# Heads sorted into slots at run time, with band-only work for five slots when at most three heads retrieve

## The chip, the cores and the metric

The kernel runs on one core of one Trainium2 chip. The metric is the device time of one execution in microseconds (us); all times below are us unless marked ns. The engines are named as the profile names them: PE is TensorE (PEld its weight loads), DVE is VectorE, ACT is ScalarE, POOL is GpSimd, and SP is the engine whose queue issues nearly all transfers.

## The reference

Attention for 4 batches and 8 heads with 768 positions of 64 elements, then a feed-forward layer on the 3072 joined rows. A head that is marked in `is_retrieval` sees all earlier positions; the others see only the first `n_sink` = 4 positions and a window of the last `window` = 64:

```python
causal = rel >= 0                                   # rel = query position - key position
stream_keep = causal & ((key < n_sink) | (rel < window))
mask = causal if is_retrieval[head] else stream_keep
a = softmax(where(mask, q @ k.T / 8, -1e9)) @ v     # per batch and head
x = a.transpose(0, 2, 1, 3).reshape(3072, 512)
out = maximum(x @ w1, x @ w2) @ w_out               # w1, w2: 512 x 1024; w_out: 1024 x 512
```

`is_retrieval` is an input and holds 1, 0, 1, 0, 0, 0, 1, 0: three of eight heads retrieve. The numbers `n_sink` and `window` are known when the program is built; the flags are not.

## The kernel before

**Attention.** Heads are worked on in pairs (`pair(b, p)`, 16 of them). A pair loads q, k and v for two heads in three transfers of 384 KB on SP's queue (L357, nine buffers `ld`), casts them to bf16 (`qb` and `vb`, on POOL for nearly all pairs), transposes q and k on PE (L373) and copies them out of PSUM as `qt` and `kz`. Scores are computed with keys on the partitions, in six steps for every head (the list `FULL`), each filling a PSUM buffer of up to 512 columns out of three (`sc`): three "near" steps that hold two key blocks next to the diagonal each, and three "far" ones. Together they are the whole causal triangle. ACT takes the exponential into `at` (L405). A head that doesn't retrieve is masked in two ways: in the far steps the bias of the exponential is -30000 unless the head retrieves (`bias_j`, and `bias_0`, which spares the first four keys); in the near steps DVE multiplies with a mask `msk` that is built for each head out of the flags (L267). So every head costs the same, whatever its flag. PE multiplies with v, 65 columns at a time (the 65th is a column of ones for the sum of the softmax, L429, PSUM `po`), DVE divides (L440, L441, into `xs`), and PE transposes the result (L452) into `xt`, which the dense part reads.

**Dense part.** It uses maximum(x w1, x w2) = relu(x (w1 - w2)) + x w2. `wd_bf` = w1 - w2 is computed once (L306), and `wm` = w2 w_out, too (transposes at L315, matmuls at L326). Per batch there are two groups of 384 rows, each with 32 matmuls "up" (L468), eight relus (L474 on ACT, L476 on DVE) into `gt`, and for each 128 rows four matmuls with `wm` (L484), eight with w_out (L490), a copy `ot` and a transfer to the output (L496).

**Order.** Nothing is ordered by hand. Each operation is entered into a plan (`Plan.op`) with a cost for each engine that can do it, its predecessors, its buffers and a priority. `Plan.schedule` then walks through time: the operation that can start first is taken, and among those that can start at the same time the one with the lowest priority number. This settles the order of instructions on each engine when the program is built. On the chip each engine goes through its list in that order and waits by semaphore where it must. Attention has low numbers, dense work has 1000 and more, so dense matmuls fill what attention leaves free.

**Constants.** The flags `ir` are loaded by ACT's queue (L240) beside the first q, k and v, and only the masks and biases depend on them (L257, L259, L261, L267).

Of the kernel before, what the change touches and what calls it, by code (L numbers as in the profile page):

```python
# [8 lines left out]
F32 = mybir.dt.float32  # L9
# [140 lines left out]
def kernel(  # L150
# [12 lines left out]
):  # L163
    nc = tc.nc
# [6 lines left out]
    scale = 1.0 / float(D) ** 0.5  # L171

# [11 lines left out]
    def tl(name, shape, dt=BF16, n=None):  # L184
        if n is None:
            return sb.tile(shape, dt, name=name, tag=name)
        return Pool([sb.tile(shape, dt, name=f"{name}{i}", tag=f"{name}{i}") for i in range(n)])

    def psum(name, n):
        return Pool([pp.tile([128, 512], F32, name=f"{name}{i}", tag=f"{name}{i}") for i in range(n)])  # L190
# [3 lines left out]
    row = tl("row", [128, 1], F32)  # L194
    causal = tl("causal", [128, 256], F32)
# [3 lines left out]
    ir = tl("ir", [128, H, 2], I32)  # L199
    nsf = tl("nsf", [128, H], F32)  # L200
    bias_j = tl("bias_j", [128, H], F32)
    bias_0 = tl("bias_0", [128, H], F32)
    msk = tl("msk", [128, H, 2, 256])
    w2_bf = tl("w2_bf", [128, KC, d_ff])
    wd_bf = tl("wd_bf", [128, KC, d_ff])
    wo_bf = tl("wo_bf", [128, FC, d_model])
    w2t = tl("w2t", [128, FC, d_model])
# [5 lines left out]
    ld = tl("ld", [128, 2, NB, D], F32, 9)  # L213
    qb_p = tl("qb", [128, NB, 2, D], BF16, 4)
    vb_p = tl("vb", [128, 2, NB, D + 1], BF16, 3)
    qt_p = tl("qt", [128, S], BF16, 3)
    kz_p = tl("kz", [128, 2, S], BF16, 3)
    at_p = tl("at", [128, 512], BF16, 12)
    rz_p = tl("rz", [128, NB], F32, 4)
    xs_p = tl("xs", [128, NB, d_model], BF16, 2)  # L220
    xt_p = tl("xt", [128, KC, S], BF16, 3)
    gt_p = tl("gt", [128, FC, GT], BF16, 2)
    ot_p = tl("ot", [128, d_model], F32, 3)
    sc_p = psum("sc", 3)
    po_p = psum("po", 2)
    mm_p = psum("mm", 3)

    P = Plan()

    def copy(e, o, i):  # L230
        if e == "ACT":
            nc.scalar.copy(out=o, in_=i)  # L232
        else:
# [4 lines left out]
    ir_handle = _dc.replace(is_retrieval.tensor, dtype=I32, shape=(2 * H,))  # L238
    ir_ap = bass.AP(tensor=ir_handle, offset=0, ap=[[0, 128], [1, 2 * H]])
    d_ir = P.op(lambda e: nc.scalar.dma_start(out=ir, in_=ir_ap.rearrange("p (h t) -> p h t", t=2)),  # L240
                {"ACT": 0.45}, prio=-100, size=0.3)
    c_rel = P.op(lambda e: nc.gpsimd.iota(rel, pattern=[[1, 256]], base=0, channel_multiplier=-1,
                                          allow_small_or_imprecise_dtypes=True), {"POOL": 0.5}, prio=-100)
    c_row = P.op(lambda e: nc.gpsimd.iota(row, pattern=[[1, 1]], base=0, channel_multiplier=1,
                                          allow_small_or_imprecise_dtypes=True), {"POOL": 0.3}, prio=-99)
    c_id = P.op(lambda e: nc.vector.tensor_scalar(
        out=ident, in0=rel[:, 0:128], scalar1=0.0, scalar2=None, op0=ALU.is_equal),
        {"DVE": 0.25}, [c_rel], prio=-50)
    c_ca = P.op(lambda e: nc.vector.tensor_scalar(
        out=causal, in0=rel, scalar1=0.0, scalar2=None, op0=ALU.is_ge), {"DVE": 0.22}, [c_rel], prio=-49)  # L250
    c_fa = P.op(lambda e: nc.vector.tensor_scalar(
        out=far, in0=rel, scalar1=float(window), scalar2=None, op0=ALU.is_ge), {"DVE": 0.22}, [c_rel], prio=-48)
    c_ns = P.op(lambda e: nc.vector.tensor_scalar(
        out=nsink, in0=row, scalar1=float(n_sink), scalar2=None, op0=ALU.is_ge), {"DVE": 0.1}, [c_row], prio=-47)
    c_f0 = P.op(lambda e: nc.vector.tensor_scalar_mul(out=far0, in0=far, scalar1=nsink),
                {"DVE": 0.3}, [c_fa, c_ns], prio=-46)
    c_nf = P.op(lambda e: nc.vector.tensor_scalar_add(out=nsf, in0=ir[:, :, 0], scalar1=-1.0),  # L257
                {"DVE": 0.1}, [d_ir], prio=-45)
    c_bj = P.op(lambda e: nc.vector.tensor_scalar_mul(out=bias_j, in0=nsf, scalar1=-NEG),  # L259
                {"DVE": 0.1}, [c_nf], prio=-44)  # L260
    c_b0 = P.op(lambda e: nc.vector.tensor_scalar_mul(out=bias_0, in0=bias_j, scalar1=nsink),  # L261
                {"DVE": 0.1}, [c_bj, c_ns], prio=-43)
    c_mk = []
    for h in range(H):
        def f(e, h=h):
            for m in range(2):
                nc.vector.scalar_tensor_tensor(  # L267
                    out=msk[:, h, m, :], in0=(far0 if m == 0 else far), scalar=nsf[:, h:h + 1],
                    in1=causal, op0=ALU.mult, op1=ALU.add)
        c_mk.append(P.op(f, {"DVE": 0.8}, [c_nf, c_f0, c_ca], prio=h + 0.3))  # L270

    init = []
    for i, t in enumerate(kz_p.tiles):
        for hh in range(2):
            init.append(P.op(lambda e, t=t, hh=hh: nc.vector.memzero(t[64 - 64 * hh:128 - 64 * hh, hh, :]),
                             {"DVE": 0.5}, prio=-40 + 30 * i))
    for i, t in enumerate(vb_p.tiles):
        init.append(P.op(lambda e, t=t: nc.gpsimd.memset(t[:, :, :, D:D + 1], 1.0),
                         {"POOL": 0.2}, prio=-40 + 30 * i))
    kz_init = init  # L280
# [3 lines left out]
    d_w = {}  # L284

    def load_weights(prio):
        for i, (name, arr, rows) in enumerate((("w2", moe_w2, KC), ("wo", moe_w_out, FC), ("w1", moe_w1, KC))):
            n = rows // 4
            for c in range(4):
                dst = w_raw[{"w1": 0, "w2": 1, "wo": 2}[name]][:, c * n:(c + 1) * n, :]  # L290
                src = arr[c * 128 * n:(c + 1) * 128 * n, :].rearrange("(c p) f -> p c f", p=128)
                d_w[name, c] = P.op(lambda e, dst=dst, src=src: nc.sync.dma_start(out=dst, in_=src),
                                    {"SP": 0.45}, prio=prio + 0.1 * i + 0.01 * c, size=0.524, rate=0.39)

    wd_ops, w2_ops, wo_ops, wm_ops, w2t_ops = [], [], [], [], []

    def prep_weights():
        for c in range(4):
            w2_ops.append(P.op(lambda e, c=c: copy(e, w2_bf[:, c, :], w_raw[1][:, c, :]),
                               {"DVE": 0.62, "ACT": 0.95}, [d_w["w2", c]], prio=40 + c))  # L300
        for c in range(4):
            wo_ops.append(P.op(lambda e, c=c: copy(e, wo_bf[:, 2 * c:2 * c + 2, :], w_raw[2][:, 2 * c:2 * c + 2, :]),
                               {"DVE": 0.62, "ACT": 0.95}, [d_w["wo", c]], prio=44 + c))
        for c in range(4):
            def f(e, c=c):
                (nc.vector if e == "DVE" else nc.gpsimd).tensor_sub(  # L306
                    out=wd_bf[:, c, :], in0=w_raw[0][:, c, :], in1=w_raw[1][:, c, :])
            wd_ops.append(P.op(f, {"DVE": 1.15, "POOL": 2.6}, [d_w["w1", c], d_w["w2", c]], prio=48 + c))
        for fch in range(FC):
            bk = Buf(mm_p)  # L310

            def tr(e, fch=fch, bk=bk):
                psb = bk.t.bitcast(BF16)
                for c in range(KC):
                    nc.tensor.transpose(psb[:, c * 128:(c + 1) * 128],  # L315
                                        w2_bf[:, c, fch * 128:(fch + 1) * 128], ident)
            o = P.op(tr, {"PE": 0.23}, w2_ops + [c_id], [bk], prio=300 + fch)
            w2t_ops.append(P.op(lambda e, fch=fch, bk=bk: copy(e, w2t[:, fch, :], bk.t.bitcast(BF16)[:, 0:d_model]),
                                {"DVE": 0.34, "ACT": 0.48}, [o], [bk], prio=52 + fch))
# [14 lines left out]
    def near(j):  # L334
        return (j, 128 * j, min(256, S - 128 * j), 256 * (j % 2))

    FULL = (
        ("near", [near(0), near(1)]),
        ("far0", [(0, 256, 512, 0)]),
        ("near", [near(2), near(3)]),  # L340
        ("far", [(1, 384, 384, 0), (3, 640, 128, 384)]),
        ("near", [near(4), near(5)]),
        ("far", [(2, 512, 256, 0)]),
    )

    xs, xt, xt_ops = {}, {}, {}

    def pair(b, p):
        r = b * HP + p
        h0 = 2 * p  # L350
        if p == 0:
            xs[b], xt[b], xt_ops[b] = Buf(xs_p), Buf(xt_p), []
        raws, loads = [], []
        for i, src in enumerate((q, k, v)):
            t = Buf(ld)
            raws.append(t)
            loads.append(P.op(lambda e, t=t, src=src: nc.sync.dma_start(  # L357
                out=t.t, in_=src[b, h0:h0 + 2].rearrange("h (n p) d -> p h n d", p=128)),
                {"SP": 0.45}, (), [t], prio=r + 0.01 * i, size=0.393, rate=0.225))
        bfs = []  # L360
        qt, kz, vb = Buf(qt_p), Buf(kz_p), Buf(vb_p)
        tops = []
        for i in range(2):
            t = Buf(qb_p)
            o = P.op(lambda e, t=t, i=i: copy(e, t.t.rearrange("p n h d -> p h n d"), raws[i].t),
                     {"POOL": 0.83, "DVE": 0.5} if r < 2 else {"POOL": 0.83}, [loads[i]], [raws[i], t],
                     prio=r + 0.01 * i)
            bk = Buf(mm_p)

# [131 lines left out]
    for b in range(B):  # L501
        for p in range(HP):
            pair(b, p)
# [41 lines left out]
```

The softmax here doesn't subtract the row's maximum and nothing guards it: scores larger than these inputs give would overflow.

## Time and profile before

| what | before |
|---|---|
| time, median of 3 runs (lowest to highest) | 221.69 us (221.56 to 222.52) |
| profiled execution, span | 221.9 us |
| PE busy | 199.0 us (90%), 1888 matmuls |
| ACT busy | 151.2 us (68%) |
| DVE busy | 122.7 us (55%) |
| POOL busy | 48.9 us (22%) |
| read from memory, written | 25.17 MB, 6.29 MB |
| packets under 512 bytes | 75,216 of 80,357 |

The busy time of an engine is a mean over stages with different limits. To see what bounds the kernel, the table of slices is read, in which every digit is the busy share of one fortieth of the span, then the chain of waits, which follows the work back from the last instruction, and then busy times of single stages. Rows of groups have the form: line, engine, operation, out <- in, shape, count | busy time, mean ns of one | idle time of the engine before them and what ended it. The costliest groups by their busy time are the scores at L398 (58.4), the exponentials at L405 (115.9 over all forms), the matmuls at L490 (46.5), L468 (46.3), L429 (38.5) and L484 (24.6).

### The profile page before, as it was taken

The page shows a single profiled execution, that of the slowest core. Times are in us where ns is not written, and L with a number is a line of the kernel's source. Part 1 is how long each engine was busy: PE and PEld are TensorE (multiplying, and loading weights), DVE is VectorE, ACT ScalarE, POOL GpSimd, SP SyncE. Part 2 cuts the span into 40 slices and gives each one's busy share as a digit, 9 for nine tenths or more (in the row PEclk, how much of TensorE's full clock was granted, in tenths as well). Part 3 has the DMA queues.
Part 4 walks back from the last instruction along what each step waited for, and adds up shares of the span by engine and source line. Part 5 has one row for each costly group of instructions (what it writes and reads, how often), then busy time and mean ns, then how long its engine had stood idle before and what let it go on. Part 6 is the DMA issues. An engine that isn't in the chain of part 4 may idle for free.

```text
span 221.9 us, 4796 instructions
## 1 busy us (share of the span) xinstructions
PE 199.0 (90%) x1888; PEld 125.7 (57%) x1888; DVE 122.7 (55%) x298; ACT 151.2 (68%) x291; POOL 48.9 (22%) x59
## 2 busy tenths in 40 slices
PE   0267986799999999999999999999999999999993
PEld 0245564366667677677767767755545454554541
DVE  6978999993799888988986876730000000000000
ACT  2158997675988989999989999933527253352721
POOL 1374015853542441364231100000000000000000
PEclk9999999799999999999999999999999999999999
DMA  5999999999999999999401011012021120302112
GB/s 122 219 218 316 345 321 379 227 221 198 230 212 219 206 231 241 261 226 246 75 3 47 3 47 52 0 40 96 9 97 47 47 95 4 124 17 95 47 47 95
DMA packets 80357, 31.76 MB, mean 143 GB/s; under 512 B 75216, under 2 KB 75216, under 8 KB 80336
## 3 DMA queue, kind: packets, MB, share of 16 engines
q1 hardware_dynamic: 80192, 31.46, 61.1%
q8 instruction: 14, 0.23, 0.4%
q14 instruction: 7, 0.06, 0.1%
q10 hardware_dynamic: 144, 0.01, 0.0%
HBM read 25.17 MB, written 6.29 MB: 142 GB/s over the span
## 4 chain that ended last, share of the span: by engine, by line
PE 69%; DVE 23%; ACT 3%; issue 2%; DMA 1%; ACTq 0%; DVEq 0%
PE mm L490 18%; PE mm L468 16%; PE sc L398 11%; PE mm L484 9%; PE po L429 7%; DVE at L417 4%; PE mm L326 4%; DVE msk L267 3%; DVE xs L441 3%; PE mm L373 3%; DVE kz L234 3%; DVE at L413 2%; DVE at L421 1%; DMA ir<-in_is_retrieval_dram 1%; PE mm L452 1%
## 5 line engine op out<-in xcount | busy, mean ns | idle before, releaser
L398 PE MATMUL sc<-qt,kz 128*128 128x128 bf16 (+2 forms) x320 | 58.4, 285 | 2.6 <-DVE kz L234 1.8
L405 ACT ACTIVATE at<-sc 128x512 bf16<-128x512 f32 (+1 forms) x96 | 55.3, 576 | 1.0 <-PE sc L398 0.5
L490 PE MATMUL mm<-wo_bf,gt 128*128 128x512 bf16 x192 | 46.5, 379 | 0.0
L468 PE MATMUL mm<-xt,wd_bf 128*128 128x384 bf16 x256 | 46.3, 326 | 0.0
L429 PE MATMUL po<-vb,at 128*128 128x65 bf16 x672 | 38.5, 195 | 4.1 <-DVE at L417 1.7
L429 PEld LDWEIGHTS <-at 128*128 128x128 bf16 x672 | 31.8, 98 | 14.5 <-DVE at L417 4.7
L405 ACT ACTIVATE at<-sc,bias_j 128x512 bf16<-128x512 f32 x64 | 38.2, 598 | 2.3 <-PE sc L398 1.9
L232 ACT COPY ot<-mm 128x512 f32<-128x512 f32 x22 | 12.9, 587 | 37.5 <-PE mm L490 37.5
L398 PEld LDWEIGHTS <-kz 128*128 128x128 bf16 x320 | 28.7, 100 | 16.8 <-issue 2.8
L234 POOL CAST qb<-ld 128x768 bf16<-128x768 f32 x32 | 29.9, 948 | 31.8 <-DMA ld<-in_q_dram 11.5
L468 PEld LDWEIGHTS <-wd_bf 128*128 128x128 bf16 x256 | 23.9, 98 | 14.7
L474 ACT ACTIVATE gt<-mm 128x384 bf16<-128x384 f32 x51 | 25.1, 493 | 5.9 <-PE mm L468 5.6
L490 PEld LDWEIGHTS <-gt 128*128 128x128 bf16 x192 | 17.9, 98 | 19.2
L373 PE MATMUL mm<-ident,qb 128*128 128x128 bf16 x192 | 17.1, 230 | 11.2 <-POOL qb L234 11.2
L484 PE MATMUL mm<-wm_bf,xt 128*128 128x512 bf16 x96 | 24.6, 379 | 0.0
L405 ACT ACTIVATE at<-sc,bias 128x512 bf16<-128x512 f32 x32 | 22.4, 700 | 1.4 <-PE sc L398 1.2
L234 POOL CAST vb<-ld 128x768 bf16<-128x768 f32 x16 | 13.7, 858 | 42.9 <-PE po L429 38.1
L373 PEld LDWEIGHTS <-qb 128*128 128x128 bf16 x192 | 12.8, 103 | 12.8 <-POOL qb L234 11.8
L417 DVE TENSOR_TENSOR at<-at,msk 128x512 bf16<-128x512 bf16 x32 | 19.2, 600 | 1.5 <-ACT at L405 1.3
L413 DVE TENSOR_TENSOR at<-at,msk 128x512 bf16<-128x512 bf16 x32 | 16.1, 503 | 6.0 <-ACT at L405 5.8
L441 DVE TENSOR_TENSOR xs<-po,rz 128x384 bf16<-128x384 f32 x32 | 17.8, 558 | 1.1
L234 DVE COPY kz<-mm 64x768 bf16<-64x768 bf16 x23 | 12.6, 547 | 3.1 <-PE mm L373 2.9
(43 smaller groups left out, 137.0 us busy)
## 6 DMA issues: line engine op xcount, KB each, us to landing
ld<-in_q_dram SPq DMA_DIRECT2D x16, 384.0 KB, 6.2
ld<-in_k_dram SPq DMA_DIRECT2D x16, 384.0 KB, 6.3
ld<-in_v_dram SPq DMA_DIRECT2D x16, 384.0 KB, 6.3
out_dram<-ot SPq DMA_DIRECT2D x24, 256.0 KB, 2.0
raw<-in_moe_w_dram SPq DMA_DIRECT2D x8, 512.0 KB, 6.7
raw<-in_moe_w_out_dram SPq DMA_DIRECT2D x4, 512.0 KB, 8.6
ir<-in_is_retrieval_dram ACTq DMA_DIRECT2D x1, 8.0 KB, 3.3
```

The source lines that it names most:

```text
L234: (nc.vector if e == "DVE" else nc.gpsimd).tensor_copy(out=o, in_=i)
L373: nc.tensor.transpose(psb[:, n * 128:(n + 1) * 128], t.t[:, n].rearrange("p h d -> p (h d)"), ident)
L398: nc.tensor.matmul(sc.t[:, off:off + w], lhsT=kz.t[:, hh, j * 128:(j + 1) * 128], rhs=qt.t[:, q0:q0 + w], start=True, stop=True, skip_grou ...
L405: nc.scalar.activation(out=at.t[:, 0:n], in_=sc.t[:, 0:n], func=ACT.Exp, scale=scale, bias=bias)
L413: nc.vector.tensor_mul(out=a, in0=a, in1=m)
L417: nc.vector.tensor_mul(out=a, in0=a, in1=m)
L429: nc.tensor.matmul(po.t[:, i * (D + 1):(i + 1) * (D + 1)], lhsT=at.t[:, off + t * 128:off + (t + 1) * 128], rhs=vb.t[:, hh, j, :], start=( ...
L441: nc.vector.tensor_tensor(out=xs[b].t[:, :, h * D:(h + 1) * D], in0=p3[:, :, 0:D], in1=rz.t.unsqueeze(2).to_broadcast([128, NB, D]), op=AL ...
L468: nc.tensor.matmul(bk.t[:, 0:GT], lhsT=wd_bf[:, c, f * 128:(f + 1) * 128], rhs=xt[b].t[:, c, g * GT:(g + 1) * GT], start=(c == 0), stop=(c ...
L474: nc.scalar.activation(out=gt.t[:, f, :], in_=bk.t[:, 0:GT], func=ACT.Relu)
L484: nc.tensor.matmul(bk.t, lhsT=xt[b].t[:, c, c0:c0 + 128], rhs=wm_bf[:, c, :], start=(c == 0), stop=False)
L490: nc.tensor.matmul(bk.t, lhsT=gt.t[:, f, t * 128:(t + 1) * 128], rhs=wo_bf[:, f, :], start=False, stop=(f == FC - 1))
```

## The change

The change uses the flags to leave work out, and not only to mask it. A head that doesn't retrieve needs only the blocks around the diagonal and the first four keys. Since the flags are known at run time only, the program holds two versions of the whole work and picks one with a branch.

- **Sorting.** DVE counts the flags and computes a permutation `perm` that puts the heads that retrieve first. Each engine reads the count into a register and branches (`tc.If(few <= FULL_SLOTS)`, FULL_SLOTS is 3).
- **At most three retrieve.** Slots 0 to 2 do the full triangle; slots 3 to 7 do the band alone, in three steps with smaller blocks (`BAND`: 448, 384 and 320 columns), and their four sink keys in one step of 512 columns for both heads of a pair. SP reads the eight head numbers into registers. The load of a pair becomes one transfer per head with the address from a register, and so do the loads of w1 and w2, whose rows are put into the order of the slots: 64 rows each.
- **More than three.** The full triangle for all heads, with loads by pair as before. It is not run with these flags.
- **Around it.** w_out is loaded ahead of the branch; the flags are loaded by SP's queue. The relu outputs and `w2t` lie in the memory of the raw weights, which makes room. `at` has eight buffers rather than twelve, and the band steps have `as` with three each. The exponentials are chained, so that their planned order is kept. The matmuls with w_out come ahead of those with `wm` in the dense part. Copies of sink keys and values for the band heads are made on POOL.

```diff
+    FULL_SLOTS = 3
+    narrow = window <= 64 and 0 < n_sink <= 32
+    WN = 192
...
+        nc.sync.dma_start(out=ir, in_=ir_ap.rearrange("p (h t) -> p h t", t=2))
+        for c in range(4):
+            load_weight("wo", c)
...
+        V.tensor_scalar(out=irn, in0=ir, scalar1=0.0, scalar2=None, op0=ALU.not_equal)
+        V.tensor_tensor(out=flag, in0=irn[:, :, 0], in1=irn[:, :, 1], op=ALU.max)
+        V.tensor_tensor_scan(out=count, data0=one, data1=flag, initial=0.0, op0=ALU.mult, op1=ALU.add)
...
+            V.tensor_reduce(out=perm[:, 0:H], in_=hot, axis=mybir.AxisListType.X, op=ALU.add)
+        V.tensor_copy(out=perm[:, H:H + 1], in_=nr)
...
+        BAND = (
+            ("band0", [(0, 0, 256, 0), (1, 128, WN, 256)]),
+            ("band1", [(2, 256, WN, 0), (3, 384, WN, 256)]),
+            ("band2", [(5, 640, 128, 0), (4, 512, WN, 128)]),
+        )
...
+                if rows:
+                    two = []
+                    for hh in range(2):
+                        two.append(P.op(lambda e, t=t, src=src, hh=hh: nc.sync.dma_start(
+                            out=t.t[:, hh], in_=src[b, bass.ds(head(s0 + hh), 1)].rearrange(
+                                "o (n p) d -> p (o n) d", p=128)),
+                            {"SP": 0.5}, (), [t], prio=r + 0.01 * i, size=0.197, rate=0.225))
...
+                o = score_op([(0, 256, S - 256, 0)], lambda j: ks.t, qt, [ks], tops + [ok], 2 * r + 0.15, sc)
+                o = exp_op(sc, ats, lambda t: t, S - 256, None, [o], 2 * r + 0.15)
...
-                o = P.op(d0, {"PE": 0.865}, xt_ops[b] + wm_ops, [bk, xt[b]], prio=1000 + 100 * b + 10 * g + 5 + t)
...
+                    o = P.op(d0, {"PE": 0.865}, [o] + xt_ops[b] + wm_ops, [bk, xt[b]],
+                             prio=1000 + 100 * b + 10 * g + 3 + t)
...
+    few = nc.values_load(perm[0:1, H:H + 1], min_val=0, max_val=H,
+                         skip_runtime_bounds_check_because="a count of H flags")
+    with tc.If(few <= FULL_SLOTS) as branch:
+        _, at = nc.values_load_multi_w_load_instructions(
+            perm[0:1, 0:H], engines=(mybir.EngineType.SP,), min_val=0, max_val=H - 1,
+            skip_runtime_bounds_check_because="a permutation of the heads")
+        run([s < FULL_SLOTS for s in range(H)], lambda s: at[s], True, flags_by_slot)
+    with branch.Else():
+        run([True] * H, lambda s: s, False, flags_by_head)
```

## The prediction, on record before the run

> **What bounds the kernel now.** I read the table of slices first, then the chain of waits, then busy time by stage. In the slices (40 of 5.55 us; one digit is the busy share in tenths):
>
> ```profile
> PE   0267986799999999999999999999999999999993
> ACT  2158997675988989999989999933527253352721
> DMA  5999999999999999999401011012021120302112
> ```
>
> TensorE is full from slice 10 to the end, the loads stop after slice 19, and ScalarE is nearly full until slice 26. The chain gives the stage borders: the first dense matmul starts at 53.65, and only matmuls follow at the end. From the timeline and the last pieces of the chain (start us, us, what):
>
> ```profile
> 53.65 0.81 PE L468 MATMUL mm<-xt,wd_bf 128*128 128x384 bf16 x4
> ```
>
> ```profile
> 205.16 5.20 PE mm L468 x32
> 210.36 0.86 PE mm L484 x4
> 211.22 1.73 PE mm L490 x8
> ...
> 218.21 0.58 ACT ot L232
> ```
>
> So there are three stages: up to 53.65 (attention of batch 0 and preparing weights, at the pace of the loads), 53.65 to 147 (attention mixed with dense work), 147 to 218.2 (dense alone); then 3.7 for the last copy and its transfer. Busy us by stage (length, then PE, PEld, DVE, ACT, POOL):
>
> ```profile
> 0.00:53.65 53.65, 36.60 (x397) 24.14 (x398) 47.51 (x104) 34.24 (x63) 23.06 (x29) 0.97 1.12 260
> 53.65:147.00 93.35, 91.26 (x1121) 65.47 (x1120) 73.92 (x192) 86.81 (x171) 25.87 (x31) 1.00 0.69 140
> 147.00:218.25 71.25, 71.13 (x374) 36.09 (x372) 1.25 (x3) 29.61 (x58) 0.00 (x0) 1.00 0.16 63
> ```
>
> A busy PE is not yet a PE at its peak, so I price matmuls by the chain instead: four of 384 columns take 0.65, four of 512 take 0.865, 42 of 65 take 1.29, six transposes 0.335. Each is columns / 2.4 GHz plus 2 to 4 ns. By the order in the program the mixed stage holds 1118 matmuls with 200,440 columns: 83.5 us, plus 1118 x 2.7 ns = 86.5. It lasts 93.35, so **7 us of it are stalls**. The last stage holds 374 with 168,704 columns: 70.3 + 1.0 = 71.3 of 71.25. After 53.65 the kernel is bound by TensorE's columns.
>
> [...] The queue SP shows both faces of that, an issue into an empty queue and one held back:
>
> ```profile
> 0.74 0.43 SPq L357 DMA_DIRECT2D ld<-in_q_dram  x1
> ...
> 59.74 1.69 SPq L357 DMA_DIRECT2D ld<-in_q_dram  x1
> 61.52 1.68 SPq L357 DMA_DIRECT2D ld<-in_k_dram  x1
> ```
>
> A load of 384 KB comes every 1.78; issuing needs 0.43 of it. The rest is the pace of the transfers.
>
> **The change, part by part.**
>
> 1. Fewer columns. is_retrieval has three ones, so the branch with three full slots runs. A full head has 10 score matmuls (2688 columns) and 21 for the output (L429); a band head 6 (1152 columns) and 15; each of the three pairs with a band head adds one of 512 for the sinks. Scores: 320 to 12x10 + 20x6 + 12 = 252, 86,016 to 32,256 + 23,040 + 6,144 = 61,440 columns. Output: 672 to 12x21 + 20x15 = 552, 7,800 columns fewer. Together 32,376 / 2400 + 188 x 2.7 ns = 14 us less PE. That which falls after the first dense matmul is gain; that before lies in the loads' shadow.
>
> 2. ScalarE. Exponentials go from 192 (115.9 us by the sum of rows at L405) to 144: 72 full ones at the same mean of 604 ns = 43.5, sixty band ones taken at 0.56, 0.50 and 0.49 (rows of 512, 384 and 256 give the bounds 0.61 and 0.49) = 31, twelve of 512 for the sinks = 7.3; 82. Beside that six more copies of kz at 0.79. In the mixed stage the rows add up to 112 before (87 of exponentials, the rest relus and copies) where the stage shows 86.8 busy, since the rows' durations overlap: a factor of 0.77. After, they add up to 86 (58 of exponentials from the middle of pair 4 on, 15 copies of kz, xt and qt, 18 relus, six ot): 66 busy of a stage of 76. ScalarE goes from 93% to 87% and doesn't take over.
>
> 3. VectorE. Masks: 128 products to 108 shorter ones; ten fewer of the msk instructions (10 x 0.47 = 4.7 us at the start), 11 small ones more for sorting the heads, smk and zeroing, which lie between the branch and the landing of pair 0's k (about 6 us of VectorE work in a gap of 7). GpSimd gets 48 copies of four columns or partitions and about ten clears; it was busy 26 of 93 in the mixed stage, which hides them.
>
> 4. The start. Loads of q, k and v now wait for the flags. ir landed at 4.0; then 11 dependent small VectorE instructions (nsf, bias_j, bias start 0.20 apart; the three of 64 elements taken at 0.25, between the 0.17 of 8 elements and the 0.35 of 256) = 2.4; then SP reads a register, branches, and reads eight more. No row shows such a read. [...] **first load at 8.5**, range 7.5 to 11, against 0.74. Queued behind it on SP is every load, behind those everything. w_out (2 MB) fills the wait: at the 340 GB/s of the slices it needs 6.2.
>
> 5. The way to the first dense matmul. In the built order it stands behind the transposes of pair 5's q and k (before: of pair 4's). Before, 17 loads and 6.3 MB of weights come first: 0.74 + 17x1.78 + 18.5 + 2 for landing = 51.5; the cast of pair 5's k did start at 51.19. After: 8.5 + 17x1.78 + 4.2 MB / 343 GB/s = 12.2, + 2 = 53.0. Cast 0.83, transposes 0.5 and 12 short matmuls: **first dense matmul at 55**. w1's differences and wm lie before that: w1 lands near 39, two differences at 2.4 on GpSimd end near 44.
>
> 6. The issue. 48 loads become 96 halves, 8 of w1 and w2 become 16, each with a register address and one register instruction more. The stream has 0.89 per half. The static issue of 0.43 is the lower bound; twice that plus the register work, 1.2, the upper. I take 0.6, hidden.
>
> 7. The mixed stage. 918 matmuls with 162,190 columns: 67.6 + 2.5 = 70.1, plus stalls between 0 (ScalarE is freer) and 15 (shorter bursts, each with its own chain of score, exponential, mask, output); I take 6: **76**. Pair 15's k stands 59 us into the stage, near 114; it lands by 8.5 + 12.2 + 47x1.78 + three stores at 1.7 + 2 = 111.5. The loads end just in time.
>
> 8. The last stage. 390 matmuls with 175,872 columns: 73.3 + 1.0 = **74.3**. L490's matmuls now come ahead of L484's, so at the last group nothing stands between the last relu and its reader: one relu (0.49) and its signals, 1.
>
> Sum: 55 + 76 + 74.3 + 1 + 3.7 = **210.0 us**, 5.3% below 221.69.
>
> **The rivals.**
>
> - Stalls grow: with half-filled bursts the order planned ahead fits less, and the mixed stage has 15 us of stalls. 55 + 85 + 74.3 + 1 + 3.7 = 219. For it: loads end just in time, three score buffers stay. Against it: ScalarE and VectorE have more room than before.
> - Stalls vanish: 55 + 70 + 74.3 + 3.7 = 203. For it: ScalarE at 93% was the likeliest cause of the 7 us. Against it: PE's order is fixed, and any late transfer stops it.
> - The issue becomes the bound: at 1.2 per half the first dense matmul comes at 8.5 + 50x1.2 + 2 + 2 = 72.5, and pair 15 is 10 pairs x 6 x 1.2 = 72 behind pair 5 rather than 59, so 72.5 + 89 + 74.3 + 1 + 3.7 = 240, **slower**. The break-even is near 1.03 per half. For it: no register-addressed DMA is in this trace. Against it: the bare issue takes less than half of the room.
>
> **How the numbers follow.** Main case 0.57 (206 to 214), stalls grow 0.20 (214 to 222), stalls vanish 0.10, issue as the bound 0.13 (part of it between 222 and 240). Range 202.5 to 221: it leaves out the slow issue and the edges of the second and third. Faster 0.85, same 0.02, slower 0.13.
>
> **What would show it.** Right: the first row of L541 on SP at 8 to 9; pitch of the halves near 0.89 with short issues when the queue is empty; the first up matmul (L616) near 55; 252 score and 552 output matmuls in the page; the last output matmul near 131; then dense alone for 74 us. Wrong: halves over 1 us apart with the DMA slices below 9 (the issue binds); PE digits of 7 and 8 in the mixed stage with waits for exponentials or masks (stalls); a first load after 11 (the register reads are mispriced).

## The result, and the profile after

The changed kernel takes **219.29 us** (median of four runs, 218.64 to 220.31) against 221.89 for the kernel before beside it (221.56 to 222.52): a ratio of 0.988, 95% interval 0.984 to 0.993. The forecast was 210.0. The direction was right and the time lies in the range, but the gain is 1.2% where 5.3% had been forecast. Medians and ratios here are of fast executions alone; the one profile of a slow one is that of e6_two_queues (228.37 us at a mean granted clock of 0.944, where its fast ones took 223.41 to 226.70 at 0.961 to 0.962), so its landmark in the table below may be late for that reason too.

First the table of slices, now 40 of 5.46 us; PEclk is the TensorE clock that was granted, in tenths, and GB/s what the transfers moved:

```profile
PE   0029767699789999998999999999999999999990
ACT  0738878335988989977899887625426263442621
PEclk9999995769999999999999999999999999999999
DMA  5999999999999999999995111012021120202121
GB/s 170 307 221 219 221 232 235 225 181 223 219 199 225 206 230 191 221 240 225 232 247 121 51 48 52 0 54 96 0 96 48 51 96 32 113 4 96 48 89 67
```

Counting slices from 0, TensorE's digit is only 6 or 7 in slices 4 to 7 (22 to 44 us), and its granted clock drops to 0.5 to 0.7 in slices 6 to 8 (33 to 49 us). The DMA engines read as busy all the time up to slice 20; their digit doesn't show at which rate they work. GB/s does: w1 and w2 are on their way in slices 4 to 7, at 221 to 235 (in e1_full below, the same weights at full width come at 357, at a DMA share of 1.02 against 1.06 here). Next, from the timeline, the first dense matmul, which the forecast had put at 55 (start us, us, what):

```profile
62.52 0.81 PE L617 MATMUL mm<-xt,wd_bf 128*128 128x384 bf16 x4
```

and busy us by stage, with borders set as in the forecast, at the first dense matmul and at the last matmuls of the attention (length, then PE, PEld, DVE, ACT, POOL, granted clock, DMA share, GB/s):

```profile
0.00:62.52 62.52, 38.52 (x393) 25.76 (x394) 37.96 (x103) 38.91 (x68) 26.37 (x51) 0.92 1.10 223
62.52:139.00 76.48, 73.06 (x914) 53.18 (x912) 63.23 (x163) 65.75 (x134) 33.01 (x67) 1.00 0.83 171
139.00:213.70 74.70, 74.62 (x398) 38.00 (x396) 1.31 (x3) 31.06 (x62) 0.00 (x0) 1.00 0.16 61
```

The mixed stage lasts 76.5 (forecast 76), the last one 74.7 (forecast 75.3). So the miss lies ahead of 62.52. The queue SP there (issue start, us in which it was issuing; by the page, a load lands 4.3 to 4.4 after its issue and a half of w1 or w2 8.3, in the median):

```profile
7.62 0.98 SPq L541 DMA_DIRECT2D ld<-in_q_dram  x2
...
20.89 2.11 SPq L541 DMA_DIRECT2D ld<-in_v_dram  x2
23.18 14.14 SPq L366 DMA_DIRECT2D raw<-in_moe_w_dram  x16
38.07 1.37 SPq L541 DMA_DIRECT2D ld<-in_q_dram  x2
40.30 4.95 SPq L541 DMA_DIRECT2D ld<-in_k_dram  x2
```

The sixteen halves of w1 and w2 hold the queue for 14 us, and pair 3's k cannot be issued to its end before 45.25. What follows is seen on GpSimd, whose casts mark when each load has landed (in brackets: idle before it, and what ended that):

```profile
39.13 2.35 POOL L384 TENSOR_TENSOR wd_bf<-raw 128x1024 bf16<-128x1024 f32 x1 [9.56 <-DMA raw<-in_moe_w_dram]
43.65 2.35 POOL L384 TENSOR_TENSOR wd_bf<-raw 128x1024 bf16<-128x1024 f32 x1 [2.17 <-DMA raw<-in_moe_w_dram]
47.06 0.82 POOL L255 CAST qb<-ld 128x768 bf16<-128x768 f32 x1 [1.06 <-DMA ld<-in_q_dram]
...
60.18 0.90 POOL L255 CAST qb<-ld 128x768 bf16<-128x768 f32 x1 [0.99 <-PE mm L563]
```

The first two rows are half of the differences w1 - w2, the last two the casts of pair 3's q and pair 5's k. VectorE takes the other half, and its last difference waits for the last part of w1 until 45.59 (its timeline):

```profile
45.59 1.50 DVE L384 TENSOR_TENSOR wd_bf<-raw 128x1024 bf16<-128x1024 f32 x1 [1.61 <-DMA raw<-in_moe_w_dram]
```

From pair 3's q on a cast follows each 1.8 us, the pace of the loads. Pair 5's k is cast at 60.18, where the forecast had 53.0, and the first dense matmul comes 2.3 later, where it had 2.0. So of the 7.5 us by which the first dense matmul is late, 7.2 lie in the loads.

### The profile page after: what moved, and what is told of

Its sections match the earlier page's. It is cut to its first block, busy times and chain, and to the rows that moved or that the text cites. A ratio compares the mean times of both kernels' runs of the same rounds, so it can differ in the third digit from the quotient of the medians.

```text
span 218.5 us, 4707 instructions
## 1 busy us (share of the span) xinstructions
PE 186.2 (85%) x1700; PEld 116.9 (54%) x1700; DVE 102.5 (47%) x269; ACT 136.3 (62%) x262; POOL 59.4 (27%) x117
## 4 chain that ended last, share of the span: by engine, by line
PE 56%; DVE 11%; DMA 11%; SPq 8%; ACT 5%; issue 4%; POOL 2%; ACTq 0%; POOLq 0%; DVEq 0%
PE mm L636 17%; PE mm L617 16%; PE mm L642 9%; DMA raw<-in_moe_w_dram 7%; SPq L541 7%; PE sc L435 6%; PE po L507 3%; DVE as L451 3%; DVE kz L255 3%; PE mm L563 2%; ACT at L442 2%; ACT kz L253 2%; DMA ld<-in_v_dram 2%; DVE at L451 2%; DMA ir<-in_is_retrieval_dram 1%
## 5 line engine op out<-in xcount | busy, mean ns | idle before, releaser
L636 PE MATMUL mm<-wo_bf,raw 128*128 128x512 bf16 x192 | 46.3, 379 | 0.0
L435 PE MATMUL sc<-qt,kz 128*128 128x256 bf16 (+3 forms) x240 | 41.2, 270 | 5.4 <-ACT at L442 2.3
L442 ACT ACTIVATE as<-sc 128x384 bf16<-128x384 f32 (+3 forms) x72 | 32.3, 517 | 4.5 <-PE sc L435 4.3
L624 ACT ACTIVATE raw<-mm 128x384 bf16<-128x384 f32 x55 | 27.1, 492 | 9.0 <-PE mm L617 8.7
L636 PEld LDWEIGHTS <-raw 128*128 128x128 bf16 x192 | 18.3, 98 | 20.1 <-issue 0.6
L451 DVE TENSOR_TENSOR as<-as,smk 128x448 bf16<-128x448 bf16 (+2 forms) x60 | 24.0, 436 | 5.6 <-ACT as L442 5.5
L451 DVE TENSOR_TENSOR at<-at,msk 128x512 bf16<-128x512 bf16 (+2 forms) x48 | 19.2, 428 | 4.3 <-ACT at L442 4.2
L442 ACT ACTIVATE at<-sc 128x512 bf16<-128x512 f32 (+1 forms) x36 | 20.5, 569 | 0.3 <-PE sc L435 0.2
L255 POOL CAST vb<-ld 128x768 bf16<-128x768 f32 x16 | 13.4, 838 | 19.1 <-DMA ld<-in_v_dram 8.9
L507 PE MATMUL po<-vb,at 128*128 128x65 bf16 x252 | 15.2, 195 | 2.6 <-DVE at L451 2.4
L507 PEld LDWEIGHTS <-at 128*128 128x128 bf16 x252 | 12.5, 99 | 5.3 <-DVE at L451 4.0
```

Of the source, the lines that this page charges most:

```text
L255: (nc.vector if e == "DVE" else nc.gpsimd).tensor_copy(out=o, in_=i)
L435: nc.tensor.matmul(sc.t[:, off:off + w], lhsT=lhsT(j), rhs=qt.t[:, q0:q0 + w], start=True, stop=True, skip_group_check=True)
L442: nc.scalar.activation(out=view(at.t), in_=view(sc.t), func=ACT.Exp, scale=scale, bias=0.0 if bias is None else bias)
L451: V.tensor_mul(out=a, in0=a, in1=m)
L507: nc.tensor.matmul(po.t[:, i * (D + 1):(i + 1) * (D + 1)], lhsT=at.t[:, off + t * 128:off + (t + 1) * 128], rhs=vb.t[:, hh, j, :], **flag_ ...
L624: nc.scalar.activation(out=gt.t[:, f, :], in_=bk.t[:, 0:GT], func=ACT.Relu)
```

## The experiments

Unless it is said otherwise, an edit is to the changed kernel. Five runs leave work out and compute something else (e1, e2, f1, g1, n1), s1 holds for this input alone, and e0_rates, which stands outside the table, only moves data. Two landmarks tell more than the run times: the first dense matmul, and what lies behind it up to the end of the span. In the nine runs that keep the changed kernel's planned order (the first nine rows), the second is 154.5 to 156.2 us. Single times of the kernel before, taken anew beside each group of runs, spread from 220.8 to 228.3 us, so mainly the landmarks decide. A landmark comes from one profiled execution; for the changed kernel, profiled twice, the two lie 0.3 us apart.

| run | first dense matmul, us | behind it, us | median time, us |
|---|---|---|---|
| changed kernel | 62.5 | 156.0 | 219.29 |
| a0_unchanged | 62.2 | 156.2 | 219.94 |
| e1_full | 60.4 | 155.9 | 218.28 |
| e2_halves_fixed | 62.4 | 154.7 | 218.83 |
| e6_two_queues | 70.9 | 155.7 | 226.33 |
| f1_no_pool_wd | 56.7 | 156.0 | 214.66 |
| g1_short_wm | 58.3 | 155.6 | 215.36 |
| n1_halves_no_pool_wd | 63.6 | 155.3 | 220.82 |
| s1_no_branch | 62.0 | 154.5 | 218.67 |
| h1_gather | 68.6 | 155.9 | 226.27 |
| e7_pair3_first | 49.0 | 174.4 | 225.2 |
| k1_wd_vector | 62.9 | 157.3 | 222.76 |
| m1_natural_order | 62.1 | 158.1 | 221.5 |
| m2_both | 57.9 | 158.3 | 218.0 |
| m3_natural_wd_late | 58.6 | 158.3 | 219.48 |
| e4_full_triangle | 73.7 | 165.7 | 241.7 |

**1. The transfers by themselves.** My theory A, a guess that no trace had shown yet: a transfer into 64 partitions runs at about half the rate of one into 128. The rivals: the register address (B), or the size of 256 KB (C).

```diff
+    def full(name, i, arr, c):
+        nc.sync.dma_start(out=w_raw[i][:, c, :], in_=arr[128 * c:128 * c + 128, :])
+    def columns(name, i, arr, c):      # two of 128 x 512
+    def halves(name, i, arr, c):       # two of 64 x 1024
+    def registers(name, i, arr, c):    # the same, arr[bass.ds(at[2 * c + hh], 1)]
+    def two_queues(name, i, arr, c):   # the same, odd halves by nc.scalar
```

> The two weights w2 and w1 (4.19 MB) are loaded five times in a row, each time after a VectorE copy has read the ones before; nothing else runs (the kernel computes nothing and writes zeros). Five forms: 128 partitions in 8 transfers; 128 partitions by 512 columns in 16 transfers; 64-partition halves in 16 transfers with fixed addresses; the same halves with the address from a register; the same halves with fixed addresses, odd ones on ScalarE's queue. Theory A (a transfer into 64 partitions gets half the rate, and two that stand in one queue hardly run beside each other): about 12, 12 to 13, 20, 20 and 12 to 13 us. Rival B (an address from a register makes the transfer slow): 12, 12, 12, 20, 12 us. Rival C (transfers of half the size, eight of them in flight, are slow whatever partitions they go to): 12, 20, 20, 20, 20 us or a little less for the last.

A small copy on VectorE marks the landing of each of the two matrices (2.10 MB), form after form. The lines shown are the full width (w2, w1), the end of the columns (w1), the fixed halves (w2, w1) and the halves by register (w2):

```profile
9.39 0.17 DVE L307 COPY gate<-raw 128x8 f32<-128x8 f32 x1 [7.93 <-DMA raw<-in_moe_w_dram]
14.51 0.17 DVE L307 COPY gate<-raw 128x8 f32<-128x8 f32 x1 [4.94 <-DMA raw<-in_moe_w_dram]
...
26.82 0.17 DVE L307 COPY gate<-raw 128x8 f32<-128x8 f32 x1 [6.72 <-DMA raw<-in_moe_w_dram]
35.67 0.17 DVE L307 COPY gate<-raw 128x8 f32<-128x8 f32 x1 [8.68 <-DMA raw<-in_moe_w_dram]
44.39 0.17 DVE L307 COPY gate<-raw 128x8 f32<-128x8 f32 x1 [8.54 <-DMA raw<-in_moe_w_dram]
53.12 0.17 DVE L307 COPY gate<-raw 128x8 f32<-128x8 f32 x1 [8.55 <-DMA raw<-in_moe_w_dram]
```

Full width: 2.10 MB in 14.51 - 9.39 = 5.1 us, 410 GB/s. By columns, 128 partitions and 256 KB each: 12.3 us for both. Halves at fixed addresses: 17.6 for both, 2.10 MB in 8.7, 240 GB/s. Halves by register: w2 in 53.12 - 44.39 = 8.7 as well. So B is out, and C explains a small part at most (4.19 MB in 12.3 us by columns are 341 GB/s, between 410 and 240). A holds, with 240 of 410, somewhat more than half. Why a transfer into 64 partitions is slower, no run here shows. A's last number was wrong: two queues. There the fifth form's w2 ran beside the fourth's w1, and the page of slices (2.43 us each) has 209 to 241 GB/s from 53 to 75 us, no more than one queue has (238 to 243 from 27 to 53 us). The 397 to 407 at the end is the writing of the output.

```profile
GB/s 83 373 277 405 417 399 385 388 388 359 195 238 240 238 243 241 240 240 243 243 238 243 241 221 213 216 228 214 209 216 218 241 270 397 405 407 407 407 340 70
```

**2. Full-width and fixed halves in the kernel.**

```diff
-                    for hh in (range(2) if rows else (None,)):
+                    for hh in (None,):                                # e1_full
-                                    in_=arr[bass.ds(head(2 * c + hh), 1)].rearrange("o d f -> (o d) f"))
+                                    in_=arr[2 * c + hh])              # e2_halves_fixed
```

> The changed kernel, but w1 and w2 come in 8 transfers of 128 partitions with fixed addresses, as before the change; their rows are then not in slot order, which leaves the sorting of the weights out of what is computed. Theory A (half-partition transfers cost the lost 8 us): about 211 us, first dense matmul at about 55 us, last w1 landing by 38 us. Rival B (addresses from registers): about 211 too. Rival C (size and number): about 211 too. Rival D (the weights aren't the cause, the in-order GpSimd and the order of the loads are): 218 to 219 us.

> The changed kernel, w1 and w2 as sixteen halves of 64 partitions as in the change, but at fixed addresses in natural order (the sorting of the weights' rows is left out of what is computed). Theory A: 218 to 220 us, as the changed kernel, weights at 200 to 235 GB/s. Rival B (addresses from registers): about 211 us. Rival C: 218 to 220. Rival D: 218 to 219.

e2 comes out as the changed kernel (62.4): the register address costs nothing here either. In e1 the weights do run as they did before the change; the windows of 24 to 44 in the changed kernel and 24 to 36 in e1 have

```profile
24.00:44.00 20.00, 13.85 (x167) 10.58 (x168) 13.42 (x35) 13.43 (x27) 6.20 (x10) 0.83 1.06 231
```

```profile
24.00:36.00 12.00, 8.92 (x126) 6.55 (x126) 10.39 (x27) 10.44 (x23) 4.83 (x9) 1.00 1.02 357
```

Pair 3's q is cast at 40.84 instead of 47.06, so 6 us of the loads are won, but the first dense matmul comes only 2 us earlier, at 60.4. My figure of 55, and 211 for the run, fell (it took 218.28): another wait had stood right behind the loads. VectorE's and GpSimd's timelines of e1 show it:

```profile
33.99 3.89 DVE L451 TENSOR_TENSOR as<-as,smk 128x448 bf16<-128x448 bf16 x6
...
39.19 2.15 DVE L384 TENSOR_TENSOR wd_bf<-raw 128x1024 bf16<-128x1024 f32 x1
```

```profile
35.30 2.41 POOL L384 TENSOR_TENSOR wd_bf<-raw 128x1024 bf16<-128x1024 f32 x1 [5.36 <-DMA raw<-in_moe_w_dram]
37.91 2.35 POOL L384 TENSOR_TENSOR wd_bf<-raw 128x1024 bf16<-128x1024 f32 x1 [0.21 <-DMA raw<-in_moe_w_dram]
```

Six band masks take 3.89, and a difference on VectorE 2.15 that runs in about 1.2 elsewhere; it ends 1.1 after GpSimd's. In these traces the masks grow from 1.69 in the changed kernel, where GpSimd has nothing beside them (36.00 to 37.69), to 3.89 where its differences run (35.30 to 40.26). That the differences hold VectorE up is theory F of the next runs. In the changed kernel the weights come so late that GpSimd's differences (39 to 46) miss these masks; with faster weights they fall right on them.

**3. Is that it, or TensorE's own queue?** Two cuts on top of e1.

```diff
+                n = d_ff if e == "DVE" else 8                         # f1: GpSimd's two differences
+                    out=wd_bf[:, c, 0:n], in0=w_raw[0][:, c, 0:n], in1=w_raw[1][:, c, 0:n])
...
+                        nc.tensor.matmul(bk.t[:, 0:64], lhsT=..., rhs=wo_bf[:, f, 0:64], ...)   # g1
```

> The run with w1 and w2 in full-width transfers at fixed addresses (e1_full), and GpSimd's two differences w1 - w2 cut from 1024 to 8 columns (the rest of wd is zero, so the dense part computes something else); every engine's order stays. Theory F (GpSimd's 2.4 us differences hold VectorE's two-input instructions up, and VectorE is what the way to the first dense matmul waits for between 27 and 43 us): six band masks near 34 us take 2 to 2.6 us instead of 3.89, VectorE's differences about 1.2 instead of 2.15 and 1.61, first dense matmul at 56 to 58 instead of 60.4, run near 215. Rival G (TensorE's own queue, the product w2 x w_out ahead of pair 3, is the wait): first dense matmul at 60 or later, run 218.

> The run with w1 and w2 in full-width transfers at fixed addresses (e1_full), and the product w2 x w_out (32 matmuls at L404) cut from 512 to 64 columns (the rest of wm is zero); every engine's order stays. It takes 32 x 0.19 = 6 us of TensorE's work away ahead of pair 3's transposes. Theory G (TensorE's queue from 43.5 to 60.4 is full, so its work there counts in full): first dense matmul at 54 to 55.5, run near 213. Theory F (VectorE): first dense matmul at 58 to 60, run 216 to 218. If the loads of pair 5 bind (its k was cast at 53.9): not before 55.

f1's VectorE, and then g1's:

```profile
35.14 1.87 DVE L451 TENSOR_TENSOR as<-as,smk 128x448 bf16<-128x448 bf16 x6
```

```profile
33.88 6.64 DVE L451 TENSOR_TENSOR as<-as,smk 128x448 bf16<-128x448 bf16 x6
```

The same six masks take 1.87 without GpSimd's differences, and 6.64 in g1, where these start at 33.83 and so a moment ahead of them. f1 has its first dense matmul at 56.7, 3.7 earlier than e1. It clears wd on GpSimd at the start, which moved its first load from 7.63 (e1) to 8.98. But that isn't a handicap any more when pair 3's q lands, since the weights took longer in e1's profiled execution (pair 3's q cast in e1, f1 and g1):

```profile
40.84 1.18 POOL L255 CAST qb<-ld 128x768 bf16<-128x768 f32 x1 [0.58 <-DMA ld<-in_q_dram]
40.81 0.82 POOL L255 CAST qb<-ld 128x768 bf16<-128x768 f32 x1 [2.73 <-DMA ld<-in_q_dram]
39.50 0.83 POOL L255 CAST qb<-ld 128x768 bf16<-128x768 f32 x1 [0.60 <-DMA ld<-in_q_dram]
```

So f1's 3.7 us arise behind equal loads. The masks behave as theory F says, and the first dense matmul lies in F's range; how much of the 3.7 is the granted clock stays open (see "What stays open" below). g1 is at 58.3, but its pair 3 landed 1.3 earlier than e1's, so it can't be set against e1's 60.4 as it is. From the start of pair 3's first transposes to the first dense matmul e1 needs 14.0 (46.46 to 60.42) and g1 12.0 (46.34 to 58.34). So the shorter matmuls are worth some 2 there, and TensorE's queue counts too: F against G was not an either-or.

**4. Does GpSimd cost anything in the changed kernel itself?** The same cut with the half-width weights, and a version that leaves nothing out, with all differences on VectorE.

```diff
-            wd_ops.append(P.op(f, {"DVE": 1.15, "POOL": 2.6}, ...))
+            wd_ops.append(P.op(f, {"DVE": 1.15}, ...))                # k1_wd_vector
```

> The changed kernel with its half-width weights, and only GpSimd's two differences cut from 1024 to 8 columns (the rest of wd is zero), all orders as they are. If the half-width weights alone set the first dense matmul here and GpSimd's work is hidden behind them (the differences run at 39 to 46, after the masks of pair 2, and pair 3's q has not landed when they end): first dense matmul at 61 to 62.3, run 218.5 to 220. If GpSimd's differences cost here what they cost with full-width weights (3.7 us): 58.5, run 216.

> The changed kernel with nothing left out; the four differences w1 - w2 may go to VectorE only (before: VectorE or GpSimd), and the order is planned anew. VectorE gets 2 x 1.2 us more, GpSimd loses 2 x 2.35 us that stood ahead of pair 3's casts and waited for w1. Theory F (GpSimd's differences hold VectorE's masks up) with the half-width weights as before: first dense matmul at 58.5 to 60.5, run 215.5 to 217.5. If only the loads matter: 62 and 219.

> The changed kernel itself, beside the three runs below on the same chip: 218.5 to 220 us, first dense matmul at 62 to 63.

No. n1 has 63.6, and its first load, too, is late by 1.4 because of the clearing, which leaves pair 5's k 1.1 late (cast at 61.27 against 60.18):

```profile
8.99 0.98 SPq L541 DMA_DIRECT2D ld<-in_q_dram  x2
```

From that cast to the first dense matmul it takes 2.3, as in the changed kernel. k1 brings no gain (62.9; 222.76 us): pair 3's q is still cast at 46.83, when it has landed. As long as the weights are half-width, they hide GpSimd's part. The forecast for k1 failed because I had added a gain to a bound that it doesn't touch.

**5. The start.** The order of the heads written into the program, no branch, no registers.

```diff
-    with tc.If(few <= FULL_SLOTS) as branch:
+    order = (0, 2, 6, 1, 3, 4, 5, 7)
+    run([s < FULL_SLOTS for s in range(H)], lambda s: order[s], True, flags_by_slot)
```

> The changed kernel without branch and registers: the order of the heads 0, 2, 6, 1, 3, 4, 5, 7 is written into the program, so it holds for this input alone; the loads of q, k, v no longer wait for the sorting and stand behind w_out in the queue. Prices the step of the start: the first load issues near 3 instead of 7.6, but w_out's 2 MB in front need until about 9, so pair 0's q lands some 2 us earlier. First dense matmul at 59.5 to 61, run 216.5 to 218.5. If the 4.6 us of the issue counted in full: 58, run 214.5. If the loads are bound elsewhere: 62 and 219.5.

```profile
3.18 1.31 SPq L541 DMA_DIRECT2D ld<-in_q_dram  x2
```

```profile
11.55 0.82 POOL L255 CAST qb<-ld 128x768 bf16<-128x768 f32 x1 [7.51 <-DMA ld<-in_q_dram]
```

In the changed kernel the same cast, of pair 0's q, is at 11.81:

```profile
11.81 1.05 POOL L255 CAST qb<-ld 128x768 bf16<-128x768 f32 x1 [2.41 <-DMA ld<-in_q_dram]
```

The loads are issued 4.4 us earlier and land 0.3 earlier, since w_out's 2 MB stand ahead of them. Sorting, branch and register reads cost the path some 0.3 us (first dense matmul 62.0, against 62.2 and 62.5 in the changed kernel). I had expected 2.

**6. Other ways to bring the weights.** Odd halves by ScalarE's queue; pair 3 ahead of the weights; rows gathered by GpSimd's indirect transfers, 128 partitions at a time.

```diff
+                                (nc.sync if hh == 0 else nc.scalar).dma_start(                 # e6
...
-        dw = weights(2.5)
+        dw = weights(3.5)                                                                     # e7
...
+                                nc.gpsimd.indirect_dma_start(                                  # h1
+                                    out=w_raw[...][:, c, :], out_offset=None, in_=...,
+                                    in_offset=bass.IndirectOffsetOnAxis(ap=idx[:, c:c + 1], axis=0))
```

> The changed kernel with nothing left out; the eight halves of w1 and w2 that go to partitions 64 to 127 are issued by ScalarE on its own queue instead of by SyncE, in the same places of the order; all other engines' orders stay. ScalarE pays about 8 x 0.5 us of issue, where it is busy 38.5 of 62.5 us. Theory A: two queues fill both halves of the partitions at once, so 212 to 215 us with the first dense matmul at 56 to 58 us, if ScalarE's in-order waits don't hold its issues back. Rival B: 218 to 220 us, since the addresses still come from registers. Rival D: 218 to 219.

> The changed kernel with nothing left out; only the priority of the loads of w1 and w2 is 3.5 instead of 2.5, so pair 3's q, k, v come ahead of them. If the half-width weights in front of pair 3 are what leaves TensorE idle from 38 to 44, pair 3 fills that hole: first dense matmul at 58 to 60, run 215 to 217. If the weights' preparation itself (VectorE, GpSimd, TensorE after their landing) is the wait, it only moves later: first dense matmul at 62 to 64, run 218 to 221.

> The changed kernel with nothing left out; the rows of w1 and w2 come by 8 indirect transfers of GpSimd (512 KB each, 128 partitions, one row index per partition, worked out on VectorE in five small instructions after the sorting) instead of 16 halves on SyncE. Theory A: the weights get 300 GB/s and more, pair 3 no longer stands behind them, first dense matmul at 57 to 60 if an issue costs GpSimd about 1 us; run 214 to 217. If the issue costs 2 us and more each, pair 2's casts behind it on GpSimd wait: first dense matmul at 65 and run over 221.

All three are slower than the kernel before: ratios of 1.014 (1.007 to 1.021), 1.010 (1.006 to 1.013) and 1.015 (1.006 to 1.024). In e6 ScalarE issues its eight halves from 17.45 to 30.28 and SyncE its first at 29.98, so they hardly ran as pairs. Beside ScalarE's halves pair 2 came late (its v issued at 26.87, against 20.89 in the changed kernel), and the run's 60 band masks took 28.4 in sum, against 24.0 there. That GpSimd's differences met some of them is my reading.

```profile
29.98 12.29 SPq L366 DMA_DIRECT2D raw<-in_moe_w_dram  x8
```

In h1 an issue costs GpSimd about 0.94, with 0.3 between two; four of them put pair 2's casts, at 24.16 in the changed kernel, to 29.91, and GpSimd's differences then run into the masks as in e1 (three of them take 3.46 beside the difference at 41.71).

```profile
28.97 0.94 POOL L370 DMA_INDIRECT raw<-in_moe_w_dram,idx  x1 [0.30 <-issue]
29.91 1.60 POOL L257 CAST qb<-ld 128x768 bf16<-128x768 f32 x2
```

e7 starts the dense part at 49.0 and then stops in it: TensorE's dense matmuls stand in its fixed order before wd is ready (waits of e7 from 49 to 90: us in total, times, longest). That wait and one of 1.2 for VectorE's part of wd explain 3.5 us; what else makes e7 slow was not taken apart.

```profile
PEld L617 <- POOL wd_bf L384: 2.3, 1, 2.3
```

**7. Both repairs, nothing left out.** Weights unsorted at full width, and each head's output written to its natural columns instead; then also the differences on VectorE.

```diff
-                V.tensor_tensor(out=xs[b].t[:, :, s * D:(s + 1) * D], in0=p3[:, :, 0:D],
+                V.tensor_tensor(out=xs[b].t[:, :, bass.ds(head(s) * D, D)] if rows else ...,
...
+            if p == HP - 1:                       # a batch's transposes of xs after its last pair
+                for x in range(HP):
+                    transposed(b, x, list(all_norms))
...
+            wd_ops.append(P.op(f, {"DVE": 1.15}, ...))                # m2 beside that
```

> The changed kernel with nothing left out; w1 and w2 come unsorted in 8 full-width transfers at fixed addresses, and VectorE writes each head's output straight to its natural columns of xs, at an offset from a register (32 such instructions), so that x needs no sorted weights; a batch's four transposes of xs then wait for its last pair. Weights at 360 GB/s and more as in e1_full, VectorE and GpSimd still in each other's way: first dense matmul at 60 to 62, run 217.5 to 219.5. If the register offsets cost VectorE 0.5 us each: 16 us more on an engine that is not the bound for most of the run, up to 222.

> The last two together, nothing left out: weights unsorted in full-width transfers, differences on VectorE only. If the two causes are what the forecast missed, they add up: first dense matmul at 56.5 to 58.5, run 213.5 to 216. If one hides behind the other: no better than the better of the two.

> Nothing left out. The kernel that takes w1 and w2 unsorted in full-width transfers (m1_natural_order), with GpSimd's two differences handed to VectorE after its own two, where VectorE had idled from 46 to 50; all else in place. First dense matmul at 57.5 to 59 instead of 62.1, and as there 158 us behind it: run 216.5 to 218.

m1 alone, with the differences still on GpSimd, is at 62.1 and not faster than the kernel before (ratio 0.997, 0.994 to 1.001). With both, the first dense matmul is at 57.9 (m2, masks 1.74) and 58.6 (m3), as expected: neither repair alone gains, both together gain 4. But 158.3 us lie behind it instead of 156, so 2 of them are lost again in the later transposes or the register offsets; which of the two was not tried. m2's 218.0 us (0.976 of the kernel before, 0.967 to 0.984) is the best that leaves nothing out, beside 219.94 for the changed kernel measured with it. All three runs took 1.5 to 2 us longer than was expected of them.

**8. The branch without the band.**

```diff
-    with tc.If(few <= FULL_SLOTS) as branch:
+    with tc.If(few <= 2) as branch:
```

> The changed kernel with the condition of the branch set to at most two heads, so that this input takes the other side: full triangles for all eight heads, loads by pair at fixed addresses, full-width weights, behind the sorting and the branch. It has the 14 us of TensorE columns back, about 8 us of them after the first dense matmul. By the forecast's sums without the band gain: 220 to 225, first dense matmul at 53 to 57.

241.7 us, ratio 1.089 (1.074 to 1.105): far outside what I expected. Part of it is the start: VectorE's first instruction on this side of the branch waits 5.19 us, against 0.49 on the side that the flags take.

```profile
5.91 0.34 DVE L295 TENSOR_SCALAR far<-far,nsink 128x256 f32<-128x256 f32 x1
11.45 0.17 DVE L662 TENSOR_SCALAR nsf<-flag 128x8 f32<-128x8 f32 x1 [5.19 <-issue]
```

The rest, up to a first dense matmul at 73.7, I did not take apart. The wide side has 165.7 us behind the first dense matmul, 2.6 less than the kernel before (221.9 - 53.6 = 168.3), so its whole loss lies ahead of it. The narrow side gains 22 us over the wide one of the same program, but only 2.6 over the kernel before.

## Why the prediction was right or wrong, point by point

- **Steps 1, 2, 6, 7 and 8 hold.** 252 score and 552 output matmuls; ScalarE 65.75 busy in the mixed stage (66); stages of 76.5 and 74.7. The halves' issues take 0.47 for the weights and are hidden: loads from pair 3 on keep a pace of 1.8 per q, k or v. The rival of a binding issue fell, and so did the one of growing stalls: 76.48 - 73.06 leaves 3.4 in which TensorE isn't busy.
- **Step 4 was near.** First load at 7.62, forecast 8.5. The sorting ended at 6.19, and the nine register reads, the branch and the first address took 1.4 after it, where 2.1 had been taken, an estimate that no trace had shown. What I had not worked out is that the size of this step scarcely matters, with w_out ahead in the queue: s1 shows 0.3 us.
- **Step 5 failed**, in its term "4.2 MB / 343 GB/s = 12.2". By the formula pair 2's v lands at 8.5 + 9 x 1.78 + 2 = 26.5, and e1 has its cast at 26.50 (by some luck, as its loads start 0.9 earlier than the formula's). In the changed kernel that cast is at 27.76, 1.3 later beside the halves, and the last part of w1 comes at 45.59, 19.1 after 26.5. I took the rate of full-width transfers for transfers into 64 partitions; alone these get 240 GB/s against 410. With 19.1 for 12.2 the formula gives 59.9 for pair 5's k, and 60.18 was measured. I had not looked at what the change does to the shape of a transfer.
- **A second limit lay hidden behind it.** Repairing that term alone gives 60.4, not 55, because differences on GpSimd then meet the masks on VectorE. With both out of the way f1 reaches 56.7. Of the 7.5 us, about 2 come back with the first repair and some 4 only with the second after the first; the two can't be added in the other order (n1 and k1: nothing). The rest is open.
- **GpSimd was priced by its own time alone.** Step 3 says that it hides its copies, and step 5 lets its differences end near 44 at no cost to others. That is true of GpSimd's own time, not of what VectorE's masks take beside it (3.89 in e1, 1.69 without). In this kernel it cost nothing, because the late loads hid it.
- **The sum is a span, and was set against a time.** Its stages come from a profile of 221.9 whose execution took 223.88; the changed kernel's 218.5 belongs to one of 220.31. So 210.0 would be about 212 as a time. As spans, the miss of 8.5 is 7.5 up to the first dense matmul, 0.5 in the mixed stage, -0.6 in the last and 1.1 behind it (4.8 where 3.7 had been taken).
- **What stays open.** The granted clock was 0.92 up to the first dense matmul in the changed kernel, 0.94 in e1 and 1.00 in f1. TensorE's busy time there is 38.5, 36.8 and 34.8, so up to 2 us of what f1 gained over e1 may be clock. The same holds for m2 and m3 (0.97 and 1.00) over m1 (0.92). What lowers the clock, no run here shows.

## What to carry to other kernels

Look at the partitions of every transfer that a change reshapes: one that fills 64 partitions had 240 GB/s where 128 had 410, the DMA busy digits don't show it (9 at either rate in e0_rates), and two in turn, in one queue (240) or two (209 to 241), don't make up for it. When a bound is removed, ask what stands within a few us behind it: here each of two repairs gained 2 us or nothing alone, and 4 together without any work left out. Before giving GpSimd a job, check what VectorE has to run beside it: six masks took 3.89 and 6.64 beside GpSimd's differences, where they took 1.69 to 1.87 without; and in the changed kernel a mask of 320 columns that starts with a cast on GpSimd at 58.4 took 0.99, where one at 32.30, with GpSimd idle, took 0.32.

## What the runs showed of the hardware that was not expected

- The masks grow a lot: six of 320 to 448 columns took 1.87 us without differences of full size on GpSimd, and 3.89 (e1) or 6.64 (g1) with two of 2.35 to 2.43, which started 1.3 after the masks in e1 and 0.05 ahead of them in g1.
- Register addresses cost a transfer no rate (8.7 us for 2.10 MB either way).
- The two sides of the branch start differently: 0.49 us until VectorE's first instruction on the one, 5.19 on the other.
- A clearing of 3.6 us on GpSimd, at the start of f1 and n1, moved the first load by 1.4 us, although GpSimd was done with it before the branch. The chains show where: the comparison that makes `causal` on VectorE (L277), ahead of the sorting, has 2% of the span in both, 3 to 5 us, where it takes 0.28 in the changed kernel. In g1, which clears `wm`, half as much, the first load is at 7.67.
